# The product of k^T v and the output weights, from full-array matmuls to sixteen 32x32 array tiles in four quarters

## The chip, the cores and the metric

The kernel runs on one core of one Trainium2 chip. The metric is the device time of one execution in microseconds. It is a little longer than the "span" of a profile (1637.31 against 1635.5 us for the profiled run of the changed kernel), which runs from the first to the last instruction. The block that the change touches is computed twice in one execution, so an effect of 1 us in one such layer shows as 2 us in the time.

## The reference

The input x has 2048 rows and 1024 columns, in bfloat16. Two blocks alternate, A, B, A, B, each on a layer norm of x and added back to x. Block B is a gated product of three large matmuls and isn't touched. Block A is linear attention with 32 heads of 32 columns:

```
q, k, v = split(x @ wqkv)                  # 32 heads, Dh = 32
phi(t)  = where(t > 0, t + 1, exp(t)) + 1e-6
kv      = einsum("bhsd,bhse->bhde", phi(k), v)     # 32 x 32 for each head
z       = sum of phi(k) over the rows
o       = (phi(q) @ kv) / (phi(q) . z + 1e-6)
return  o @ wo
```

## The kernel before

The kernel uses that (phi(q) kv) wo = phi(q) (kv wo). For each layer A it forms M = kv wo once, a 1024x1024 matrix, and then one output unit for each of 16 row tiles multiplies normalised phi(q) by M. kv is block diagonal: one 32x32 block for each head, four heads in each 128x128 chunk, eight chunks. The kernel before cuts the blocks out with a mask and multiplies each whole 128x128 chunk, of which three quarters are zeros, by 128 rows of wo. PE is TensorE, DVE is VectorE and ACT is ScalarE in the profile's lines.

To keep PE busy while M is evicted from PSUM, M is formed between the steps of the last q unit (row tile 15). A q unit is 16 full matmuls followed by `phi`: ScalarE does exp and relu from PSUM, VectorE then does a minimum and a sum (`sum_up`). The list `later` holds a `sum_up` that is put off.

```python
def kv_unit(m):                                    # last step, m == 7
    ...
    for h in range(2):
        nc.vector.tensor_tensor(out=KVb[:, 4*h:4*h+4, :], in0=acc[0][:, 4*h:4*h+4, :],
                                in1=mask[:].unsqueeze(1).to_broadcast([P, 4, P]), op=ALU.mult)

def q_with_m(t, later):
    pss = [psum.tile([P, 2, NB], F32, tag="kv", bufs=1, name="pm"), mm_tile()]
    ps = mm_tile()                                 # q unit 15 itself
    pss.append(mm_tile())
    for c in range(KD):                            # eight chunks
        pm = pss[(0, 1, 0, 2, 1, 0, 2, 0)[c]]
        both(pm, KVb[:, c, :], wo[c], True, True)  # two matmuls 128x512
        if c % 2:  nc.scalar.copy(out=M[:, c, :], in_=flat(pm))
        else:      nc.vector.tensor_copy(out=M[:, c, :], in_=flat(pm))
        both(ps, xT[...][:, c, ...], wq[:, c, :], c == 0, c == KD - 1)
        if c == 2:
            do(later)
    phi(ps, q_slot(t), scale_of(t))
...
q[6] = q_unit(14, later)
do(... + [g[7], kv[6], q[5], kv[7], q[6]])         # q[5] is q unit 13
q_with_m(15, later)
do([out_unit(0)] + d(13) + ...)
```

The kernel has four PSUM slots here: three with the tag "mm" and one with the tag "kv". So the product has three slots in rotation (`pss`), the q unit has the fourth, and the output units take over the "mm" slots in the order in which they were handed out.

## Time and profile before

| | |
|---|---|
| time, median of 2 runs | 1631.2 us (1630.58 to 1631.82) |
| span of the profiled run | 1629.3 us |
| PE busy | 1615.8 us, 99% of the span |
| chain that ended last | 99% PE |
| 32 product matmuls, both layers, at 0.216 us | 6.9 us, 0.42% of the time |

The engines' busy times on the page of the kernel before, with share of the span and number of instructions:

```profile
PE 1615.8 (99%) x7498; PEld 741.0 (45%) x7649; DVE 609.1 (37%) x889; ACT 289.3 (18%) x387; POOL 55.1 (3%) x141
```

PEld is the weight loads, one for each matmul. There are 151 more of them than matmul records: some matmul records are missing from this trace.

The timeline of the kernel before around the product of the first layer A (start in us, length in us, engine, line, operation; in brackets the idle time just before and what ended it):

```profile
173.26 1.28 DVE L308 TENSOR_TENSOR KVb<-kv,mask 128x512 bf16<-128x512 f32 x2
174.60 0.60 PE L202 MATMUL pm<-W,KVb 128*128 128x512 bf16 x2 [0.27 <-remote]
175.04 0.59 PE L202 MATMUL ps<-W,xT 128*128 128x512 bf16 x2
175.25 1.23 DVE L324 CAST R<-pm 128x1024 bf16<-128x1024 f32 x1 [0.70 <-PE pm L202]
175.48 0.59 PE L202 MATMUL ps<-W,KVb 128*128 128x512 bf16 x2
...
178.29 0.42 DVE L211 TENSOR_SCALAR e<-e 128x1024 bf16<-128x1024 bf16 x1
178.81 0.69 DVE L212 TENSOR_TENSOR PQ<-PQ,e 128x1024 bf16<-128x1024 bf16 x1
...
181.27 0.59 PE L202 MATMUL ps<-W,xT 128*128 128x512 bf16 x2
181.70 10.52 PE L202 MATMUL ps<-R,xT 128*128 128x512 bf16 x47
```

PE starts a pair of matmuls every 0.43 us, product and q in turn, from 174.60 until the first output unit begins at 181.70. The evictions (L324, and L322 on ScalarE) hide behind it. The one wait that the profile shows is 0.27 us, for the masked blocks. Most of it is a matmul of q unit 14 whose record is missing (15 records for 16 weight loads): that unit ends at about 174.55, and PE stood still for some 0.05 us. VectorE had first to do the `sum_up` of unit 13. So VectorE and ScalarE matter only where PE comes to wait for them.

### The profile page before, as it was taken

Reading aid. Unit: us, or ns where it says so; the run is one execution under the profiler, and the core shown is the slowest. Engines: PE = TensorE matmul, PEld = TensorE weight load, DVE = VectorE, ACT = ScalarE, POOL = GpSimd, SP = SyncE. Lnnn points to the kernel's source line nnn. Section 1 sums busy time; section 2 is a strip of 40 time slices with the busy share of each in tenths; the row PEclk is TensorE's granted clock in tenths of the full one; section 3 lists DMA queues with packets and bytes.
Section 4 is the critical chain, followed back from the end, with each engine's and each line's share of the span. In section 5 each row is a group of like instructions: output and inputs, shape, how many; then the busy total and the mean of one; then the engine's idle time right before and its main releaser. Section 6 shows DMA issues by size and latency. Waiting matters only on the chain.

```text
span 1629.3 us, 17583 instructions
## 1 busy us (share of the span) xinstructions
PE 1615.8 (99%) x7498; PEld 741.0 (45%) x7649; DVE 609.1 (37%) x889; ACT 289.3 (18%) x387; POOL 55.1 (3%) x141
## 2 busy tenths in 40 slices
PE   9999999999999999999999999999999999999999
PEld 4444444444444444444444444444444444444444
DVE  6789853212311321243245798432123113211111
ACT  5533201101110110011045222011011101101110
POOL 2100000000000000010000000000000000000000
PEclk9999999999999999999999999999999999999999
DMA  7324856511550452142420258455136405511400
GB/s 234 58 71 105 233 162 171 164 53 52 156 180 0 132 161 96 52 154 62 92 55 1 78 104 233 155 175 161 65 91 176 140 20 173 164 65 65 155 0 27
DMA packets 235742, 182.82 MB, mean 112 GB/s; under 512 B 101264, under 2 KB 216464, under 8 KB 235664
## 3 DMA queue, kind: packets, MB, share of 16 engines
q1 hardware_dynamic: 235664, 181.69, 38.8%
q8 instruction: 60, 0.98, 0.3%
q14 instruction: 18, 0.15, 0.0%
HBM read 153.09 MB, written 4.19 MB: 97 GB/s over the span
## 4 chain that ended last, share of the span: by engine, by line
PE 99%; issue 1%; DMA 0%; SPq 0%; DVE 0%; another core or an unknown queue 0%
PE ps L202 50%; PE ps L480 47%; PE ps L507 1%; PE kv L303 0%; DMA W<-in_A_wqkv_dram 0%; PE pm L202 0%; SPq L107 0%; PE pt L365 0%; DVE X L488 0%
## 5 line engine op out<-in xcount | busy, mean ns | idle before, releaser
L480 PE MATMUL ps<-xT,R 128*128 128x512 bf16 x2379 | 525.7, 379 | 2.8
L480 PEld LDWEIGHTS <-R 128*128 128x128 bf16 x2432 | 238.0, 98 | 286.9
L484 DVE TENSOR_TENSOR R<-gs,ps 128x512 bf16<-128x512 f32 x224 | 153.9, 687 | 533.5 <-ACT gs L483 533.5
L202 PEld LDWEIGHTS <-R 128*128 128x128 bf16 x2248 | 219.8, 98 | 264.2
L483 ACT COPY gs<-ps 128x512 f32<-128x512 f32 x224 | 131.4, 586 | 1039.1 <-PE ps L480 1016.1
L480 PE MATMUL ps<-xT,W 128*128 128x512 bf16 x1133 | 250.6, 379 | 1.0
L202 PEld LDWEIGHTS <-xT 128*128 128x128 bf16 x1536 | 149.6, 98 | 179.4 <-issue 1.5
L202 PE MATMUL ps<-W,xT 128*128 128x512 bf16 x1003 | 225.0, 379 | 2.2 <-DMA W<-in_A_wqkv_dram 1.1
L480 PEld LDWEIGHTS <-W 128*128 128x128 bf16 x1152 | 112.7, 98 | 135.9
L202 PE MATMUL ps<-W,R 128*128 128x512 bf16 x728 | 169.2, 379 | 0.6
L488 DVE TENSOR_TENSOR X<-X,ps 128x1024 bf16<-128x1024 bf16 (+3 forms) x34 | 39.4, 1158 | 335.8 <-PE ps L202 326.1
L202 PE MATMUL ps<-R,R 128*128 128x512 bf16 x499 | 112.1, 379 | 0.7
L202 PE MATMUL ps<-PQ,R 128*128 128x512 bf16 x484 | 111.5, 379 | 0.6
L202 PE MATMUL ps<-R,xT 128*128 128x512 bf16 x502 | 110.3, 379 | 0.5
L207 ACT ACTIVATE e<-ps 128x1024 bf16<-128x1024 f32 x56 | 57.4, 1024 | 145.4 <-PE ps L202 140.4
L181 DVE BATCH_NORM_STATS2 st<-X 128x6 f32<-128x512 bf16 x128 | 81.9, 681 | 2.0 <-DMA X<-in_A_x_dram 1.8
L185 POOL TENSOR_SCALAR ve<-mv 128x1 f32<-128x1 f32 x64 | 16.6, 260 | 1334.1 <-DVE mv L183 1334.1
L202 PE MATMUL ps<-xT,R 128*128 128x512 bf16 x244 | 58.4, 379 | 0.4
L202 PE MATMUL ps<-GL,R 128*128 128x512 bf16 x245 | 58.4, 379 | 0.2
L336 DVE TENSOR_TENSOR X<-X,ps 128x1024 bf16<-128x1024 bf16 x32 | 38.8, 1213 | 28.0 <-PE ps L202 27.7
L211 DVE TENSOR_SCALAR e<-e 128x1024 bf16<-128x1024 bf16 x64 | 27.0, 422 | 45.7 <-ACT e L207 45.7
L192 DVE TENSOR_SCALAR R<-X,mv,rstd 128x1024 bf16<-128x1024 bf16 x64 | 33.9, 542 | 23.9 <-POOL rstd L187 23.9
(64 smaller groups left out, 459.8 us busy)
## 6 DMA issues: line engine op xcount, KB each, us to landing
R<-in_B_w_gate_dram SPq DMA_DIRECT2D x38, 1024.0 KB, 5.3
R<-in_B_w_up_dram SPq DMA_DIRECT2D x38, 1024.0 KB, 7.4
W<-in_B_w_gate_dram SPq DMA_DIRECT2D x18, 1024.0 KB, 5.4
W<-in_B_w_up_dram SPq DMA_DIRECT2D x18, 1024.0 KB, 7.1
W<-in_A_wqkv_dram SPq DMA_DIRECT2D x10, 1024.0 KB, 6.1
W<-in_B_w_down_dram SPq DMA_DIRECT2D x6, 1024.0 KB, 11.5
PQ<-in_B_w_down_dram SPq DMA_DIRECT2D x4, 1024.0 KB, 7.9
X<-in_A_x_dram SPq DMA_DIRECT2D x15, 256.0 KB, 6.5
```

The source lines that it names most:

```text
L181: nc.vector.bn_stats(out=st[:, c, :], in_=X[:, t, c * NB:(c + 1) * NB])
L185: nc.gpsimd.tensor_scalar(out=ve[:], in0=mv[:, 1:2], scalar1=1e-5, scalar2=None, op0=ALU.add)
L192: nc.vector.tensor_scalar(out=dst, in0=X[:, t, :], scalar1=mv[:, 0:1], scalar2=rstd[:], op0=ALU.subtract, op1=ALU.mult)
L202: nc.tensor.matmul(out=ps[:, n, :], lhsT=lhsT, rhs=rhs[:, n * NB:(n + 1) * NB], start=start, stop=stop)
L207: nc.scalar.activation(out=e[:], in_=flat(ps), func=ACT.Exp, **sc)
L211: nc.vector.tensor_scalar(out=e[:], in0=e[:], scalar1=1.0, scalar2=EPS, op0=ALU.min, op1=ALU.add)
L336: nc.vector.tensor_tensor(out=X[:, t, :], in0=X[:, t, :], in1=flat(ps), op=ALU.add)
L480: nc.tensor.matmul(out=ps[:, n, :], lhsT=w[:, k, j * P:(j + 1) * P], rhs=xT[g % 2][:, k, :], start=(k == 0), stop=(k == KD - 1))
L483: nc.scalar.copy(out=gs[:], in_=ps[:, 0, :])
L484: nc.vector.tensor_tensor(out=hT[:, f, :], in0=gs[:], in1=ps[:, 1, :], op=ALU.mult)
L488: nc.vector.tensor_tensor(out=X[:, t, a:b], in0=X[:, t, a:b], in1=ps, op=ALU.add)
L507: nc.tensor.matmul(out=ps[:, 0, 0:b - a], lhsT=hT[:, f, tl * P:(tl + 1) * P], rhs=wd[f][:, a:b], start=(f == 0), stop=(f == KF - 1))
```

## The change

The intent is to multiply only the blocks. The array is used as sixteen tiles of 32x32: 16 small matmuls, one for each block of four chunks, are meant to run side by side (in the trace after, all 16 of a quarter start within 0.06 us), so that a quarter of M (four chunks, half the columns) takes about the time of one full matmul, 0.216 us, rather than of four, 0.86 us. For that, the kernel places the four blocks of one chunk in the same rows of the array, and the four that share its columns come from four chunks; VectorE places the 16 pairs of blocks with 16 small copies, and wo is loaded in the matching order.

```diff
-    KVb = const.tile([P, KD, P], BF16, tag="KVb", name="KVb")
+    KVb = const.tile([P, 2, 4, DH], BF16, tag="KVb", name="KVb")
...
+    wo_v = A_wo.rearrange("(s r j e) n -> s r e j n", s=2, r=4, j=4)     # loaded by 8 transfers, not 2
...
-                    for h in range(2):
-                        nc.vector.tensor_tensor(out=KVb[:, 4 * h:4 * h + 4, :], in0=acc[0][...], in1=mask..., op=ALU.mult)
+                    for r in range(4):
+                        for j in range(4):
+                            nc.vector.tensor_copy(out=KVb[DH * r:DH * r + DH, :, j, :],
+                                                  in_=acc[0][DH * j:DH * j + DH, r:KD:4, DH * j:DH * j + DH])
...
-            for c in range(KD):
-                (one chunk: two product matmuls, one eviction, two q matmuls; do(later) after c == 2)
+            for i in range(4):
+                h, n = i // 2, i % 2
+                pm = [pss[(2 * i + u) % 3] for u in range(2)]
+                for j in range(4):
+                    for r in range(4):
+                        nc.tensor.matmul(out=pm[r // 2][DH * j:DH * j + DH, r % 2, :],
+                                         lhsT=KVb[DH * r:DH * r + DH, h, j, :],
+                                         rhs=wo[h][DH * r:DH * r + DH, j, n * NB:(n + 1) * NB],
+                                         start=True, stop=True, tile_position=(DH * r, DH * j))
+                for u in range(2):
+                    copy = nc.scalar.copy if u else nc.vector.tensor_copy
+                    copy(out=M[:, 4 * h + 2 * u:4 * h + 2 * u + 2, n * NB:(n + 1) * NB], in_=pm[u][:])
+                for c in range(2 * i, 2 * i + 2):
+                    both(ps, xT[...], wq[:, c, :], c == 0, c == KD - 1)
+                if i == 1:
+                    do(later)
             phi(ps, q_slot(t), scale_of(t))
...
-        q[6] = q_unit(14, later)
+        q[5], q[6] = q_unit(13, later), q_unit(14, later)
```

## The prediction

> **What bounds it now.** TensorE. The page shows PE busy 1615.8 of 1629.3 us (99%), granted clock 0.9 or more in all slices; the chain that ended last is 99% PE. VectorE or ScalarE work is free unless PE waits for it. The change touches the last q unit of each of two layers (timeline, from 174.3 and 983.4 us): there PE alternates 16 product matmuls (KVb x wo, 128x512) with 16 q matmuls, one per 0.216 us, from 174.60 to 181.70 us, after a 0.27 us wait for KVb.
>
> **What the change does.**
> - Removes 16 full-array matmuls per layer: 3.45 us, 6.9 us in both (0.42%): the whole possible gain.
> - Adds 4 x 16 matmuls of 32x32 tiles. [...]
> - KVb: 16 copies of 32x64 instead of two masked 128x512 ones (683 ns each, 0.60 apart[...]). Estimate 0.14 to 0.2 us each, 2.2 to 3.2 us, under q unit 14 (3.4 us on PE). The deferred sum of unit 13 lets them start at 171.2 instead of 173.26, so the wait for KVb should vanish.
> - Both deferred sums (L211 + L212, 1.1 us each) now sit in VectorE's order between its second and third evictions of the product.
> - Evictions stay four of 1.23 us (VectorE) and four of 1.02 us (ScalarE), but come in pairs after each quarter, into three rotating PSUM tiles, with only four q matmuls (0.86 us) between quarters.
> - wo arrives by eight transfers of 256 KB instead of two; issued near 146 us, needed at 174: no effect.
>
> **The critical path (first layer, estimates from those durations).** q unit 14 ends 174.55. Quarter 0 ends 175.3; VectorE copies to 176.5, while ScalarE does unit 14's exp and relu until 176.45. Quarter 1 needs both: ends 177.3 (PE idle 0.5). VectorE copies to 178.55; quarter 2 waits for it, ends 179.3. VectorE does the two sums to 180.65 and copies quarter 2's first tile to 181.9; quarter 3 needs that slot: PE idle nearly 2 us, ends 182.6. The first output unit takes the slot that ScalarE frees at 183.65. It began at 181.70 before. So PE saves array time but waits about 3.5 us, and each layer is about 2 us longer; both about 4 us. Nothing later absorbs it, for PE is the bound.
>
> **Prediction: 1635.0 us, 8 in 10 between 1631.0 and 1640.5; faster by over 2%: 0.005, within 2%: 0.985, slower by over 2%: 0.01.**
>
> **What would show it.** PE busy falls by 4 to 7 us while the span grows. Product matmuls wait for VectorE's and ScalarE's copies; the timeline has a PE gap near 2 us before quarter 3, smaller ones before 1 and 2, none for KVb. First output unit at 183 to 184.5. The rest of the timeline is only shifted.
>
> **What would make it wrong.** Tiles that run one after another [...]: up to 12 us slower. Much faster quarters (0.4 us): about +2 us. KVb copies above 0.22 us each: PE waits before quarter 0. PE gaps that lower the clock: slower. If the evictions do not gate as I read from program order, a gain of up to 5 us.

## The result, and the profile after

The changed kernel took 1636.22 us (two runs, 1637.31 and 1635.13) against 1631.2 us. The ratio is 1.0031, with a 95% interval of 1.0011 to 1.0051. Five later runs on another occasion (f4 below) gave 1635.21 us and 1.0025. So the change costs about 4 to 5 us. The engines' busy times after:

```profile
PE 1625.6 (99%) x7745; PEld 740.0 (45%) x7745; DVE 613.9 (38%) x917; ACT 289.3 (18%) x387; POOL 54.7 (3%) x136
```

The timeline of the changed kernel at the same place (q unit 14 ends at about 174.77 here, 0.22 us later than before; that much was there before the change took effect):

```profile
171.35 3.74 DVE L307 CAST KVb<-kv 32x64 bf16<-32x64 f32 x16 [1.40 <-PE kv L300]
175.15 0.39 PE L323 MATMUL pm<-W,KVb 32*32 32x512 bf16 x2 [0.38 <-DVE KVb L307]
...
175.20 0.39 PE L323 MATMUL ps<-W,KVb 32*32 32x512 bf16 x2
175.52 1.04 PE L199 MATMUL ps<-W,xT 128*128 128x512 bf16 x4
...
176.79 0.39 PE L323 MATMUL ps<-W,KVb 32*32 32x512 bf16 x2 [0.24 <-ACT PQ L205]
...
178.60 0.42 DVE L208 TENSOR_SCALAR e<-e 128x1024 bf16<-128x1024 bf16 x1
179.12 0.69 DVE L209 TENSOR_TENSOR PQ<-PQ,e 128x1024 bf16<-128x1024 bf16 x1
179.73 0.42 DVE L208 TENSOR_SCALAR e<-e 128x1024 bf16<-128x1024 bf16 x1
180.26 0.69 DVE L209 TENSOR_TENSOR PQ<-PQ,e 128x1024 bf16<-128x1024 bf16 x1
180.87 1.22 DVE L329 CAST R<-ps 128x1024 bf16<-128x1024 f32 x1
182.14 0.39 PE L323 MATMUL ps<-PQ,KVb 32*32 32x512 bf16 x2 [1.68 <-DVE R L329]
182.53 1.89 PE L199 MATMUL ps<-W,xT 128*128 128x512 bf16 x4
184.20 8.10 PE L199 MATMUL ps<-R,xT 128*128 128x512 bf16 x33
```

Three things are to be seen. The tiles do run side by side: all 16 of a quarter start between 175.15 and about 175.21, and the next full matmul starts at 175.52, so a quarter costs PE 0.37 us from its first tile to the next full matmul, where four full matmuls took 0.86. But PE waits: 0.38 us for the 16 block copies, about half a microsecond each around quarters 1 and 2, and 1.68 us before quarter 3, for an eviction that stands behind the two sums (L208, L209) in VectorE's order. And after that wait four q matmuls last 1.89 us instead of 1.04. The table by stretches of the same trace shows why (columns: stretch, its length, busy time and instructions of PE, PEld, DVE, ACT and POOL, the granted TensorE clock, DMA share, GB/s):

```profile
179.00:180.40 1.40, 1.40 (x20) 0.40 (x7) 1.19 (x4) 1.01 (x1) 0.00 (x0) 1.00 1.10 349
180.40:182.20 1.80, 0.12 (x16) 0.06 (x13) 1.69 (x2) 0.00 (x0) 0.00 (x0) 1.00 1.10 348
182.20:183.00 0.80, 0.80 (x16) 0.27 (x16) 0.28 (x1) 0.31 (x1) 0.00 (x0) 0.64 1.11 349
183.00:184.00 1.00, 1.00 (x4) 0.38 (x3) 0.94 (x1) 0.70 (x1) 0.00 (x0) 0.50 1.10 349
184.00:185.00 1.00, 1.00 (x3) 0.30 (x2) 0.00 (x0) 0.55 (x1) 0.00 (x0) 0.50 1.10 347
185.00:186.00 1.00, 1.00 (x4) 0.40 (x3) 0.43 (x1) 1.00 (x2) 0.00 (x0) 0.58 1.10 346
186.00:187.00 1.00, 1.00 (x7) 0.43 (x5) 0.58 (x1) 0.39 (x1) 0.00 (x0) 1.00 1.10 349
```

The granted clock is 0.5 from about 182.4 to about 185.8 us, 3.4 us long, which loses 1.7 us of work. The page's row of 40 slices can't show it, for a slice is 41 us. The second layer shows the same wait of 1.68 us at 994.28 and the same half clock after it.

The sum for the first layer, from the end of q unit 14 to the first output unit: 9.4 us after (174.8 to 184.2) against 7.15 before. It is 1.5 for the four quarters in place of 3.45; waits of about 3.7 in place of about 0.2; and 0.85 because the last four q matmuls ran at half clock. Another 0.8 us is lost in the output unit that follows. Together 3.1 us for one layer, and 6.2 us for both is the difference of the two spans (1635.5 and 1629.3).

### The profile page after: what moved, and what is told of

Read it like the earlier page. It is cut to its first block, busy times and chain, and to the rows that moved or that the text cites. A ratio compares the mean times of both kernels' runs of the same rounds, so it can differ in the third digit from the quotient of the medians.

```text
span 1635.5 us, 17964 instructions
## 1 busy us (share of the span) xinstructions
PE 1625.6 (99%) x7745; PEld 740.0 (45%) x7745; DVE 613.9 (38%) x917; ACT 289.3 (18%) x387; POOL 54.7 (3%) x136
## 4 chain that ended last, share of the span: by engine, by line
PE 98%; DVE 0%; DMA 0%; ACT 0%; SPq 0%; issue 0%; DVEq 0%
PE ps L199 50%; PE ps L486 47%; PE ps L513 1%; PE kv L300 0%; DMA W<-in_A_wqkv_dram 0%; DVE R L329 0%; SPq L107 0%; ACT e L204 0%; ACT PQ L205 0%; PE ps L323 0%; DVE PQ L209 0%; DVE e L208 0%; PE pm L323 0%; PE pt L371 0%; DVE X L494 0%
## 5 line engine op out<-in xcount | busy, mean ns | idle before, releaser
L199 PEld LDWEIGHTS <-xT 128*128 128x128 bf16 x1536 | 149.7, 98 | 181.9 <-issue 8.0
L208 DVE TENSOR_SCALAR e<-e 128x1024 bf16<-128x1024 bf16 x64 | 27.0, 422 | 41.4 <-ACT e L204 41.4
```

The lines of the kernel that those rows point to most:

```text
L199: nc.tensor.matmul(out=ps[:, n, :], lhsT=lhsT, rhs=rhs[:, n * NB:(n + 1) * NB], start=start, stop=stop)
L208: nc.vector.tensor_scalar(out=e[:], in0=e[:], scalar1=1.0, scalar2=EPS, op0=ALU.min, op1=ALU.add)
```

## The experiments

The theory: VectorE's order, with both sums ahead of its third eviction, holds back the PSUM slot of quarter 3; PE idles, and the idle time lowers the clock. Rivals: the tiles and the switches between full-array and tile matmuls (mode switches) are themselves slow; the block copies are to blame; the slow matmuls come from DMA traffic or from the tiles and not from idle time. Every result was correct. The first four runs shared one set of runs of the kernel before (1630.91 us median).

### e1_sums_last: the sums after all evictions

```diff
-                if i == 1:
+                if i == 3:
                     do(later)
```

> The two deferred phi sums run after all four evictions instead of between the second and third; nothing else changes. Theory (VectorE's order holds quarter 3's PSUM slot, and the idle PE then loses its clock): the wait of quarter 3 for VectorE falls from 1.68 us to below 0.5 us, the granted clock stays 1.00 around it, the first output unit starts 3 us earlier relative to the q unit before; time about 1629.5 us, 3 us or more below the changed kernel's 1635 to 1637. Rival (the 32x32 tiles and the mode switches themselves cost the time): quarters and gaps stay, time stays within 1 us of 1636.

Measured: 1630.33 us, ratio 0.9993 (0.9981 to 1.0006), clock 1.00. Quarter 3 and the eviction that it waits for, from the timeline of its trace:

```profile
178.78 1.23 DVE L329 CAST R<-ps 128x1024 bf16<-128x1024 f32 x1 [0.62 <-PE ps L323]
179.54 0.39 PE L323 MATMUL pm<-PQ,KVb 32*32 32x512 bf16 x2
180.05 0.39 PE L323 MATMUL ps<-PQ,KVb 32*32 32x512 bf16 x2
```

Two tiles of quarter 3 start at once and the others 0.51 us later, instead of 2.07 us later (180.07 and 182.14 in the changed kernel). One moved line gives back the whole loss, with the same tiles, copies and mode switches. The rival that the tiles are slow falls; the copies are not the main cause either. The time came 0.8 us higher than expected, and the first output unit 2.4 us earlier against q unit 14 (7.05 us after its end, not 9.4), not 3 us.

### e2_fill_gap: useless full matmuls in PE's idle time

```diff
+                if i == 3:
+                    for _ in range(8):
+                        nc.tensor.matmul(out=pm[0][:, 0, :], lhsT=xT[...][:, 0, ...], rhs=wq[:, 0, 0:NB],
+                                         start=True, stop=True)
```

> Eight full-array matmuls of no use are put into the idle time of PE before quarter 3 (they write into the free slot that quarter 3 overwrites; the result stays right). Theory (an idle PE of about 1.7 us lowers the granted clock for about 3.4 us, which costs 1.7 us a layer): quarter 3 starts at the same time, but the clock stays 1.00 after it, and the time falls by about 3.3 us to 1632.5. Rival (the slow matmuls after quarter 3 come from the DMA traffic or from switching to tiles): the clock still falls to 0.5 there and the time stays at 1636.

Measured: 1633.55 us, ratio 1.0013 (1.0001 to 1.0026), clock 1.00 in all five runs, and 1.00 at the place in question:

```profile
181.00:183.00 2.00, 2.00 (x23) 0.83 (x23) 1.37 (x2) 1.03 (x2) 0.00 (x0) 1.00 1.10 347
183.00:185.00 2.00, 2.00 (x11) 0.88 (x9) 0.79 (x3) 1.83 (x2) 0.00 (x0) 1.00 1.10 349
```

More work on PE made the kernel faster than the changed one: its five runs (1633.34 to 1633.66) lie below all seven of the changed kernel (1634.54 and more), though these ran on other occasions. The DMA share is 1.10 here as there, so DMA traffic isn't what slows the matmuls. The fall of the clock is a consequence of the idle time. What remains, 2.6 us above before (1 us more than expected), is the wait itself.

### e3_no_defer: the sum of unit 13 not put off

```diff
-        q[5], q[6] = q_unit(13, later), q_unit(14, later)
+        q[6] = q_unit(14, later)
```

> The phi sum of q unit 13 is not deferred, as in the kernel before; the 16 block copies stay. Theory: the copies start 2 us later (about 173.4 instead of 171.35), so PE waits about 2.4 us for them instead of 0.38 us before quarter 0 and may lose its clock there; in exchange only one sum of 1.1 us stands before quarter 3, whose wait falls to about 0.6 us. Time 1635 to 1639. Rival (block copies are not on the critical path): time falls by about 2 us or more, since one sum less delays quarter 3.

Measured: 1636.62 us, ratio 1.0031 (1.0018 to 1.0045). The waits moved as expected, from the timeline:

```profile
173.42 3.73 DVE L307 CAST KVb<-kv 32x64 bf16<-32x64 f32 x16
177.21 0.54 PE L323 MATMUL pm<-W,KVb 32*32 32x512 bf16 x2 [2.72 <-DVE KVb L307]
183.89 0.39 PE L323 MATMUL ps<-PQ,KVb 32*32 32x512 bf16 x2 [0.55 <-DVE R L329]
```

PE's wait for the blocks is about 2.5 us in truth: one record of q unit 14 is missing in this layer, and the second layer shows 2.51. The clock fell to 0.58 and 0.57 in the two stretches of 2 us from 177 to 181 us, that is after the long wait for the blocks, and stayed 1.00 after the wait of 0.55 us. So the copies are on the critical path when they start 2 us late. Putting off the sum of unit 13 spares that wait; its new place, ahead of an eviction, is what costs (e1).

### e5_best: an arrangement meant to beat both kernels

```diff
-                            nc.vector.tensor_copy(out=KVb[...
+                            copy = nc.scalar.copy if r == 3 else nc.vector.tensor_copy
+                            copy(out=KVb[...
-                pm = [pss[(2 * i + u) % 3] for u in range(2)]
+                pm = [pss[s] for s in ((0, 1), (2, 0), (1, 2), (0, 2))[i]]
-                for c in range(2 * i, 2 * i + 2):
+                for c in ((0, 1, 2), (3, 4, 5), (6, 7), ())[i]:
-                if i == 1:
+                if i == 3:
```

> Sums last, ScalarE does 4 of the 16 block copies, quarter 3 takes PSUM slots 0 and 2 instead of 0 and 1, and the eight q steps stand as 3,3,2,0 after the quarters. Theory: no wait for the blocks, waits of 0.3 us or less before quarters 1 to 3, the layer's window 1 to 1.5 us shorter than in the kernel before; time 1628 to 1629.5 us, that is 2 to 3 us below before (0.15%). Rival (tiles and mode switches cost as much as they save): 1631 or above.

Measured: 1628.73 us, ratio 0.9985 (0.9973 to 0.9998). The time is as expected, one step isn't. The timeline:

```profile
171.65 2.80 DVE L308 CAST KVb<-kv 32x64 bf16<-32x64 f32 x12 [1.42 <-PE kv L300]
174.54 0.85 ACT L308 CAST KVb<-kv 32x64 bf16<-32x64 f32 x4 [1.40 <-DVE KVb L308]
175.44 0.39 PE L324 MATMUL pm<-W,KVb 32*32 32x512 bf16 x2 [0.59 <-ACT KVb L308]
```

ScalarE's four copies waited for all of VectorE's, so nothing ran side by side. PE waited for the blocks as before: 0.59 us by the profile, about 0.37 with the one missing record of q unit 14, against 0.38 in the changed kernel. So sharing the copies brought nothing, and the gain over e1, 1.6 us, must come from the PSUM slots and the new places of the q steps; no run separates these.

### e6_kv_early: the copies earlier instead of shared

This is e5 with all copies on VectorE again, and the last step of the accumulation of k^T v in the middle of q unit 13, not after it.

```diff
                 for k in range(KD):                       # q_unit(13, later, mid=kv[7])
                     both(ps, xT[...], wq[:, k, :], k == 0, k == KD - 1)
+                    if mid and k == 3:
+                        mid()
-... [g[7], kv[6], q[5], kv[7], q[6]])
+... [g[7], kv[6], q[5], q[6]])
```

> As e5_best, but VectorE does all 16 block copies again, and the last step of the k^T v accumulation stands in the middle of q unit 13 instead of after it, so that the copies can start about 1.7 us earlier. Theory: the copies end before q unit 14 does, PE doesn't wait for them (0.38 to 0.60 us in the changed kernel, e1 and e5), and ScalarE's exp of unit 14 is not delayed as in e5; time about 1627.7 us, 1 us below e5_best. Rival (the wait for the copies costs nothing in the end, because quarter 1 waits for the relu of unit 14 anyway): within 0.4 us of e5_best.

Measured: 1628.15 us (1627.75 to 1628.44), ratio 0.9984 (0.9971 to 0.9996), on another chip than e5, beside runs of the kernel before of 1630.75 us. The copies ran from 169.90 to 173.63 us and PE no longer waited for them. Against e5 it is 0.6 us by the medians but nothing by the ratios, so the rival isn't refuted. The wait before quarter 1 for the relu of unit 14, 0.26 us, is still there. This is the best version found: its five runs and the nine of the kernel before (1630.20 to 1631.26) don't overlap.

### e8_old_sums_last: the new order without tiles

```diff
-        q[6] = q_unit(14, later)                   # kernel before
+        q[5], q[6] = q_unit(13, later), q_unit(14, later)
-                if c == 2:
-                    do(later)
+            do(later)                              # after the loop over the chunks
```

> The kernel before, full-array product and masked blocks, with both deferred sums after all evictions: the part of the new order that needs no tiles. It tells how much of the gain of e5 and e6 is due to the tiles. Theory: only its wait of 0.27 us for the blocks goes, so 1630.3 us, 0.5 us below before; tiles are then worth the remaining 2 to 3 us. Rival (the gain of e5 is that of the order alone): 1628.5 to 1629.

Measured: 1630.51 us (1630.04 to 1630.70), ratio 0.9997 (0.9983 to 1.0011), in the same rounds as e6. So the order alone is worth 0.2 us and not resolved, and e6 is 2.4 us better than it: the tiles do pay, once their waits are gone. e6 has other changes of order too, but without tiles little is left for an order to gain: in e8's trace the 32 matmuls from 174.43 to the first output unit at 181.51 take 7.08 us, and at 0.216 us each they need 6.91. The profiled spans agree, 1628.9 us for e8 and 1626.6 us for e6.

### e7a_old_short_gap and e7b_old_long_gap: idle time without tiles

The kernel before with both sums ahead of VectorE's second eviction, and in e7b one useless operation more.

```diff
                 both(pm, KVb[:, c, :], wo[c], True, True)
+                if c == 2:
+                    do(later)                      # both sums; no later do(later)
+                    nc.vector.tensor_tensor(out=junk2[:], in0=q_slot(13), in1=zacc, op=ALU.mult)   # e7b only
```

> The kernel before without tiles, with both deferred sums ahead of VectorE's second eviction of the product, so that PE waits for a PSUM slot. Theory: a PE gap of about 1.1 us in each layer appears before the sixth product step; a gap of that length is between the 0.55 us that left the clock at 1.00 (e3, second gap) and the 1.68 us that lowered it, so either may come; without a drop 1632.5 us, with drops 1636. Rival (only tile matmuls lower the clock): no drop, 1632.5.

> As e7a with one more VectorE operation of 1.22 us and no use ahead of the second eviction. Theory: PE gap of about 2.3 us in each layer with no tile matmul anywhere, and the granted clock falls to 0.5 for about 3.4 us after it; time about 1638.5 us. Rival (the drop belongs to the tile matmuls, not to idle time): the gap comes, the clock stays 1.00, time about 1635 us.

Measured: e7a 1632.06 us, ratio 1.0008 (0.9994 to 1.0021), with a gap of 0.65 us, shorter than expected. e7b 1634.52 us, ratio 1.0023 (1.0009 to 1.0037), with this gap:

```profile
180.62 0.59 PE L202 MATMUL pm<-PQ,KVb 128*128 128x512 bf16 x2 [1.78 <-DVE R L328]
```

The clock stayed full in both layers of its profile (the trace records no change of the clock, and the matmul pairs after both gaps start 0.43 us apart), and the mean clock was 1.0 in all four of its executions. This is what the rival said, against the theory: 1.78 us of idle time here did nothing, while 1.68 us in the changed kernel lowered the clock. Either idle time alone isn't enough, or its length isn't what counts.

### f1_fill_tiles: the idle time filled with tile matmuls

```diff
+                if i == 3:
+                    for _ in range(8):
+                        (the 8 tile matmuls of quarter 3 with r < 2, into pm[0])
```

> The changed kernel with the idle time before quarter 3 filled as in e2, but with 32x32 tile matmuls: eight rounds of the 8 tile matmuls of quarter 3 that need no more than the free slot (they are then done again; the result stays right). e7b showed a PE gap of 1.78 us with no drop of the clock where no tile matmuls run. Theory A (tile matmuls don't keep the clock up, so that the changed kernel's idle time effectively runs from the last full-array matmul at 180.15 to the next at 182.53): PE is busy, yet the clock falls to 0.5 after quarter 3 and the time stays at 1635 to 1637. Theory B (they count as work; any matmul will do): clock 1.00, time about 1633 as in e2.

Measured: 1633.33 us, ratio 1.0016 (1.0001 to 1.0031), clock 1.0 in all four executions. Tile matmuls, even 8 of the 16 places at a time, keep the clock up as full matmuls do in e2. Theory A falls. The filling also shows the tiles' rate:

```profile
179.11 1.92 PE L325 MATMUL pm<-PQ,KVb 32*32 32x512 bf16 x64
180.84 0.38 PE L331 MATMUL pm<-PQ,KVb 32*32 32x512 bf16 x2
```

Eight rounds take 1.73 us from start to start, 0.216 us a round: the rate of one full matmul.

### f2_old_gap_2p4 and f3_old_gap_2p9: longer idle time without tiles

As e7b, with one more VectorE operation on half the columns (f2) or on all of them (f3).

> As e7b (no tiles), with a further half-size VectorE operation: PE gap of about 2.4 us in each layer, the time that passes in the changed kernel from the last full-array matmul before quarter 3 to the first after it. Theory A (the length of time without full-array matmuls counts): the clock falls in at least one of the two layers, time 1637 to 1639. Theory B (something about the tile phases before the gap): no drop, about 1635.7.

> As e7b with two useless VectorE operations instead of one: PE gap of about 2.9 us, near the 2.72 us after which the clock fell in e3, here with no tile matmul at all. If idle time alone is enough: the clock falls to 0.5 for some 3.4 us, time 1638 to 1640. If the drop needs tile matmuls (e3 has them after its gap): no drop, about 1636.8.

Measured: f2 1638.81 us, ratio 1.0049 (1.0034 to 1.0064), gaps of 2.51 us; f3 1638.4 us, ratio 1.0047 (1.0031 to 1.0064), gaps of 3.04 us. In f2 the clock fell in both layers of the profile; in its first layer it was 1.00 until after 181 us, 0.84 in the stretch to 182, then 0.50 until 185. No tile matmul exists in this kernel: the fall needs no tiles. In f3 the first layer had it and the second hadn't, within one execution. The stretches after the two gaps, first layer above, second below:

```profile
181.00:182.00 1.00, 0.30 (x1) 0.10 (x1) 1.00 (x2) 0.00 (x0) 0.00 (x0) 0.51 1.10 347
182.00:183.00 1.00, 1.00 (x4) 0.36 (x3) 0.77 (x1) 0.26 (x1) 0.00 (x0) 0.50 1.11 351
...
994.00:995.00 1.00, 0.00 (x0) 0.00 (x0) 1.00 (x2) 0.00 (x0) 0.00 (x0) 1.00 1.10 346
995.00:996.00 1.00, 0.95 (x5) 0.47 (x5) 1.00 (x1) 0.32 (x1) 0.00 (x0) 1.00 1.10 347
```

So even a gap of 3 us need not bring the fall. f3, whose gap is half a microsecond longer, is no slower than f2, because it had fewer falls: four in its four executions by the mean clock, against seven.

### f4_changed_again: how often the clock falls in the changed kernel

No edit.

> The changed kernel as it is, in more executions, to count how often the clock falls. e2 and f1, whose gap is filled, took 1631.2 to 1631.9 us of span with no drop; a drop of 3.4 us at half clock adds 1.7 us. If the drop comes by chance in each layer (as f3 suggests, where one layer had it and the other not in the same execution): spans stand in groups near 1632, 1633.5 and 1635.3, with a mean clock of 1.000, 0.999 and 0.998. If it always comes: all spans within 1 us of 1635.3 and clock 0.998. Median time 1635 to 1637.

Measured: 1635.21 us, ratio 1.0025 (1.0012 to 1.0039). The five spans are 1634.9 and 1634.4 us with a mean clock of 0.998, and 1632.6, 1633.4 and 1632.7 us with 0.999; the two earlier runs were 1635.5 us with 0.998 and 1633.3 us with 0.999. The profiled one with 0.998 has the fall in both layers. A fall of 3.4 us at half clock takes 0.001 off the mean clock, so 0.998 is counted as two falls and 0.999 as one: each of the seven executions had at least one; none was without, as the theory of chance would have allowed. One fall more or less, 1.7 us, accounts for most of the spread of this kernel, 2.8 us between its seven executions, where the kernel before agrees within 1.1 us in the nine runs beside e6. (Of the nine beside e1, one stands out at 1634.24 us with 0.999, so that kernel isn't quite free of it either.)

The kept traces also hint at what the chance depends on, though no run was made for it. In all four traces with two falls (changed kernel, e3, f2, f4) the falls start 812.37 us apart, which is 238 times 3.4133 us, and a fall lasts 3.413 us in the trace of the changed kernel, while the waits end 812.14 to 813.17 us apart. The rise of the clock at the start of the changed kernel is a whole number of such lengths away too: 177.49 us, or 52 of them, before its first fall. So the recorded changes of the clock lie at the marks of a grid of 3.41 us through the whole execution. Where the program lies on it differs from run to run: the first fall starts 0.28 us after the end of the wait of 1.68 us in the changed kernel (182.42 and 182.14), and 0.58 us after it in f4 (182.06 and 181.48; the 182.06 is worked out from the granted clock of 0.53 in its stretch from 182 to 183 us). When the traces are cut at these marks, PE was busy for 51% or less of the cell before each of the nine recorded falls. The second gap of f3, which had no fall, is divided by a mark at 993.40, and its two cells are 58% and 52% busy. Here are the two cells before the falls of the changed kernel, and those two of f3:

```profile
179.01:182.42 3.41, 1.73 (x34) 0.54 (x20) 2.87 (x5) 1.01 (x1) 0.00 (x0) 1.00 1.10 348
991.38:994.79 3.41, 1.73 (x21) 0.54 (x20) 2.74 (x4) 1.01 (x1) 0.00 (x0) 1.00 1.10 348
...
989.98:993.40 3.42, 1.97 (x9) 0.79 (x9) 3.28 (x5) 1.42 (x2) 0.00 (x0) 1.00 1.10 350
993.40:996.81 3.41, 1.76 (x9) 0.81 (x9) 2.93 (x4) 1.01 (x1) 0.00 (x0) 1.00 1.10 348
```

So what seems to count is how much of one cell is idle, the small waits around the quarters with the long one. This is read from the traces, not tested. What stays open is what exactly is counted and where the limit lies. e7b's place on the grid isn't recorded; its gap of 1.78 us could leave a cell only 48% busy (estimate: 1.63 of 3.41 us), and yet it had no fall. No run moved a gap along the grid on purpose.

## Why the prediction was right

The prediction was 1635.0 us (1631.0 to 1640.5), within 2% with a chance of 0.985; measured were 1636.22 and, again, 1635.21 us. The mechanism was right, but that the sum came out so near is luck: several terms were mis-sized and offset each other. With the clock kept up (e2, f1) the time is 2.6 to 2.7 us above before, near the "about +2 us" that the prediction gives for quarters of 0.4 us.

- **The bound.** "VectorE or ScalarE work is free unless PE waits for it": right. e1 does the same work in another order and is 5 us or so faster.
- **The wait before quarter 3**, "nearly 2 us" because two sums stand ahead of an eviction: 1.68 us in the trace, and e1 removes it. Right.
- **Total waiting of about 3.5 us a layer**: about 3.7. Right in the sum.
- **The first output unit "at 183 to 184.5"**: 184.20. Right, but partly because of the clock: without the fall it would be about 183.35 (estimate: 0.85 us less).
- **A quarter at 0.7 us** (181.9 to 182.6 for quarter 3 in its path): mis-sized. It was the author's assumption, for no trace at hand then showed a tile matmul. A quarter costs PE 0.37 us in the trace, up to the next full matmul. From the first start to the last end of its 16 tiles it is 0.44 us at full clock (175.15 to 175.59) and 0.65 us at half clock (e3, 179.60 to 180.25), and in a stream part of that overlaps with the neighbours. Of the 0.37 us, 0.216 us is what one round takes in f1; the other 0.15 us no run takes apart. About 0.1 us more passes before the first tile (estimate: in the second layer of e6 six q matmuls take 1.40 us up to it, from 984.89 to 986.29, and 1.30 at 0.216 us each). No run measures a switch between full-array and tile matmuls alone.
- **Block copies at 0.14 to 0.2 us, and no wait for them**: wrong. They took 3.74 us for 16, 0.23 us each, and PE waited 0.38 us. The prediction's own limit was 0.22 us. The estimate was the author's, made from two operations on 512 columns 0.60 us apart; it didn't carry over to copies of 64 columns.
- **The clock**: named as a risk but not in the sum. It costs 1.7 us for each fall, and each execution had one or two. This term made up for the faster quarters, which saved some 1.3 us a layer against the prediction (estimate: four times 0.7 less 0.37 us); that is the luck.
- **"PE busy falls by 4 to 7 us"**: not a usable check. The page says 1615.8 before and 1625.6 after, but the trace before lacks 151 matmul records and that of the changed kernel lacks none, and work at half clock counts as busy too.
- **The eight wo transfers and the mask**: no wait for a transfer stands before the tiles in the trace. Right.

The case in one sentence: the tiles made the product faster but not its evictions. Those of 1.22 us (VectorE) and 1.01 us (ScalarE) stayed what they were (1.22 and 1.01 us before), while the product of a quarter went from 0.86 to 0.37 us.

## What to carry to other kernels

When the bounding engine gets faster in one stage, list in order what the engines that free its buffers have to do there, and move everything that nobody waits for behind the evictions: one moved line was worth more here than the tiles themselves. Price an idle stretch of TensorE at its length plus, from about 1.7 us on (the shortest that brought a fall here is 1.68 us), 1.7 us for the clock that may fall with it. And judge a gain of 0.2% by a marked stretch of the trace beside the time, for two falls of the clock, 3.4 us, are as large as such a gain.

## What the runs show of the clock, the tiles and the copies

- Idle time and the clock: gaps of 1.68 us (the changed kernel, seven executions of seven with at least one fall by the mean clock) and 2.51 us (f2, both layers of its profile) brought a fall to half clock, a gap of 1.78 us did not (e7b, none in four), and one of 3.04 us had no fall in one layer (f3). A cell of 3.41 us in which PE was still busy for 51% was followed by a fall, and one with 52% wasn't. The half clock lasted 3.4 us.
- Matmuls of 32x32 tiles kept the clock up: it was 1.0 in all four executions of f1, where 64 of them filled the gap.
- A group of 16 tiles lasts 0.44 to 0.47 us from its first start to its last end at full clock, and 0.65 us at half clock (e3). In a stream it costs PE 0.37 us up to the next full matmul and about 0.1 us before its first tile (estimate from e6), and rounds of 8 ran at 0.216 us each (f1).
- A copy of a 32x64 block from PSUM on VectorE took 0.220 us (the changed kernel), and 0.23 us from start to start.
